# Attention and MLP on one core: q and k's maxima turned by VectorE and transfers from step 16 on, kv products of two units in one row

## The chip, the cores and the metric

The kernel runs on one core of a Trainium2 chip. The metric is device microseconds of that core, the median of three runs. A core has TensorE (PE in the profile; its weight loads are PEld), VectorE (DVE), ScalarE (ACT), GpSimd (POOL) and SyncE (SP), which issues most of the transfers here. Each engine runs its own instructions in order and waits on semaphores for the others.

## The reference

For each of 8 batches and 8 heads (sequence 576, head dimension 64) the reference takes a softmax of q along the head dimension and a softmax of k along the sequence, and multiplies twice; the heads side by side are the rows of an MLP with 512 inputs, 2048 inner units and a squared ReLU:

```python
q_s = softmax over d of q            # max, exp, sum along the 64 of a row
k_s = softmax over s of k            # max, exp, sum along the 576 rows
kv  = einsum('bhsd,bhse->bhde', k_s, v)
x   = einsum('bhsd,bhde->bhse', q_s, kv)        # then (B*S, H*D) = (4608, 512)
h = x @ w_in ; r = max(h, 0) ; out = (s * r * r + b) @ w_out
```

All of it is float32. Each float32 product of the MLP and of q with kv is made of three fp32r matmuls, of a high and a low part: high by high, high by low, low by high.

## The kernel before

The MLP runs in 9 blocks of 512 tokens (8 batches, and a ninth block of the 64 left-over rows of each batch), each block in 16 steps, one for each 128 inner units. `g1(t)` makes h of step t (12 matmuls of 128x512 into one PSUM buffer, L600), and from it r, gh and gl: ACT takes the ReLU (L620), DVE squares and scales (L621), ACT rounds the high part gh (L622), DVE subtracts the low part gl (L613). `g2(t)` adds step t's part to the block's four accumulators (12 matmuls of 128x512, L674); it stands one step behind `g1`, so that PE has the order h(t), acc(t-1), h(t+1), acc(t). There is one h buffer and one r buffer, and two of gh and gl.

The attention is done in units of two heads, a pair of units at a time. The first 16 steps, with the first four pairs, are ordered by hand and by a planner; the change leaves them as they are, but for two small tiles with two buffers in place of four. From step 16 on `pair(pr)` writes out one pair after the other, 12 pairs in all, two to each of six blocks; `advance` hands its stages in between the steps (`STAGES` of them to a pair, spread over the first 13 steps of a block), and a scheduler sets each engine's order from that. The x that a block's two pairs make is used a block later.

A pair of before goes through PE in seven visits: two transposes that turn k's maxima (L469, `k_turn`), two that spread them over the partitions (L476, `spread`), twenty small matmuls for kv (L301, `heads`), and for each of the two units five transposes of q (L546) and six matmuls of q with kv (L563). DVE, ACT and POOL do the maxima, the exponentials, the sums and the splits into high and low parts between them. `held()` lets a DVE operation stand no earlier than behind the last gl. The input tiles k, q and v of these pairs have one buffer each; `loads(pr + 1)` is written behind the pair and fills them as they come free.

Of the kernel before, what the change touches and what calls it, by code (L numbers as in the profile page):

```python
# [8 lines left out]
F32 = mybir.dt.float32  # L9
# [17 lines left out]
def attention_moe(ctx: ExitStack, tc: tile.TileContext, q, k, v, w_in, w_out, s, b, out):  # L27
# [54 lines left out]
    def by_head(t):  # L82
        return t[:, 0:KQ].rearrange("p (h n d) -> p h n d", h=4, d=D)
# [4 lines left out]
    def v_tile(t):  # L88
        return t.rearrange("p (h n e) -> p h n e", h=4, n=NT)
# [316 lines left out]
    def q_stream(u):  # L406
# [79 lines left out]
    def k_exp(kt):  # L486
        nc.scalar.activation(kt, kt, AF.Exp)  # L487
        nc.gpsimd.memset(kt[LEFT:P, :, NQ], 0.0)

    def pair(pr):  # L490
        us = (2 * pr, 2 * pr + 1)
        bb = us[0] // NP
        kt, qt, vt = tiles.pop(pr)
        kt, qt, vt = by_head(kt), by_head(qt), v_tile(vt)
        kts, qts = [[t[:, 2 * i:2 * i + 2] for i in range(2)] for t in (kt, qt)]

        def sm(n):
# [34 lines left out]
        yield  # L532
        def normalize(i):
            u, qe = us[i], qes[i]
            qs = small.tile([P, NT, 2], F32, name=f"qs_{u}", tag="qs")
            nc.vector.tensor_reduce(out=qs, in_=qe, axis=AX.X, op=ALU.add)  # L536
            nc.vector.tensor_scalar(qs, qs, 1e-9, None, op0=ALU.add)
            qr = small.tile([P, NT, 2], F32, name=f"qr_{u}", tag="qr")
            nc.vector.reciprocal(qr, qs)  # L539
            nc.gpsimd.tensor_tensor(out=qe, in0=qe, in1=bc(qr, [P, NT, 2, D]), op=ALU.mult)  # L540

        def transpose(i):
            u, qe = us[i], qes[i]
            qT = ps.tile([P, 1024], F32, name=f"qT_{u}", tag="big")
            for n in range(NT):
                nc.tensor.transpose(qT[:, n * P:(n + 1) * P], qe[:, n, :, :].rearrange("p h d -> p (h d)"), ident)  # L546
            qh = work.tile([P, S], F32R, name=f"qh_{u}", tag="qh")
            ql = work.tile([P, S], F32R, name=f"ql_{u}", tag="ql")
            split(qT[:, 0:S], qh, ql, nc.scalar.copy, nc.vector)
            terms = ((kvhl[:, 0, i], qh), (kvhl[:, 0, i], ql), (kvhl[:, 1, i], qh))  # L550
            return terms

        def product(i, terms):
            u = us[i]
            hp = u % NP

            HB = TB // 2
            xh, xl = x_tile(bb)
            xp = ps.tile([P, 2, 512], F32, name=f"xp_{u}", tag="big")
            halves = [xp[:, 0], xp[:, 1]]  # L560
            for a, (t, src) in enumerate(zip(halves, (slice(0, HB), slice(HB, S)))):
                for j, (lhs, rhs) in enumerate(terms):
                    nc.tensor.matmul(  # L563
                        t[:, 0:src.stop - src.start], lhs, rhs[:, src], start=(j == 0), stop=(j == len(terms) - 1)
                    )
                if a == 1:
                    keep_left(u, t[:, HB:HB + LEFT])
            hl = [t[:, hp, :].rearrange("p (a c) -> p a c", a=2) for t in (xh, xl)]
            split(xp[:, :, 0:HB], hl[0], hl[1], nc.scalar.copy, nc.vector)
# [269 lines left out]
```

## Time and profile before

| | |
|---|---|
| median of 3 runs | 901.12 us (900.09 to 901.48) |
| the profiled execution | 900.48 us, its span 898.7 us |
| PE busy | 876.0 us, 97% of the span, 4528 matmuls |
| DVE, ACT, POOL busy | 51%, 40%, 9% |
| TensorE clock granted | 0.997 of full speed |

The page gives busy time by engine, the span in 40 slices, the transfers, the chain of work that ended last, and the costliest groups of instructions with the idle time before them. The views read beside it are the windows (busy time by stretch), the chain in order of time, the timeline of a stretch, and the groups of one engine. A busy PE is modelled (matmuls overlap), so distances between starts say more than durations.

### The profile page before, as it was taken

Reading aid. Unit: us, or ns where it says so; the run is one execution under the profiler, and the core shown is the slowest. Engines: PE = TensorE matmul, PEld = TensorE weight load, DVE = VectorE, ACT = ScalarE, POOL = GpSimd, SP = SyncE. Lnnn points to the kernel's source line nnn. Section 1 sums busy time; section 2 is a strip of 40 time slices with the busy share of each in tenths; the row PEclk is TensorE's granted clock in tenths of the full one; section 3 lists DMA queues with packets and bytes.
Section 4 is the critical chain, followed back from the end, with each engine's and each line's share of the span. In section 5 each row is a group of like instructions: output and inputs, shape, how many; then the busy total and the mean of one; then the engine's idle time right before and its main releaser. Section 6 shows DMA issues by size and latency. Waiting matters only on the chain.

```text
span 898.7 us, 11364 instructions
## 1 busy us (share of the span) xinstructions
PE 876.0 (97%) x4528; PEld 721.8 (80%) x4528; DVE 459.5 (51%) x723; ACT 357.4 (40%) x564; POOL 83.6 (9%) x110
## 2 busy tenths in 40 slices
PE   4899999999999999999999999999999999999997
PEld 3577778888888888888888888888888888888886
DVE  6999975563364536353636345554545332223222
ACT  5999863342233333242334333333333322222222
POOL 1000001110020202020102002110202100000000
PEclk9999999999999999999999999999999999999999
DMA  9977211303130303030130213031300110001001
GB/s 241 305 258 240 72 39 50 80 5 81 47 80 4 80 19 109 5 80 3 48 79 18 69 47 80 4 80 47 83 4 1 50 47 1 1 1 47 1 1 47
DMA packets 82308, 57.35 MB, mean 64 GB/s; under 512 B 52944, under 2 KB 77520, under 8 KB 82128
## 3 DMA queue, kind: packets, MB, share of 16 engines
q1 hardware_dynamic: 80848, 55.52, 21.7%
q10 hardware_dynamic: 1408, 1.12, 0.4%
q8 instruction: 35, 0.57, 0.3%
q14 instruction: 17, 0.14, 0.1%
HBM read 46.14 MB, written 10.49 MB: 63 GB/s over the span
## 4 chain that ended last, share of the span: by engine, by line
PE 89%; DVE 4%; ACT 3%; DMA 2%; SPq 1%; issue 1%; ACTq 0%; DVEq 0%
PE h L600 41%; PE acc L674 41%; PE xp L563 2%; PE kv L301 2%; PE qT L546 1%; ACT low L202 1%; DMA raw<-in_q_dram 1%; DVE w L225 1%; ACT st L205 1%; DMA k<-in_k_dram 1%; PE xp L443 0%; DMA q<-in_q_dram 0%; ACT r L633 0%; DVE low L218 0%; DVE st L215 0%
## 5 line engine op out<-in xcount | busy, mean ns | idle before, releaser
L600 PE MATMUL h<-x,w 128*128 128x512 f32 x1728 | 428.9, 393 | 2.3 <-ACT r L633 1.6
L600 PEld LDWEIGHTS h<-x,w 128*128 128x128 f32 x1728 | 321.9, 188 | 70.5 <-ACT r L633 3.4
L674 PE MATMUL acc<-w,gh 128*128 128x512 f32 x1152 | 340.6, 392 | 0.0
L674 PEld LDWEIGHTS acc<-w,gh 128*128 128x128 f32 x1152 | 215.1, 188 | 44.3 <-ACT o L687 0.4
L621 DVE SCALAR_TENSOR_TENSOR r<-r,sb 128x512 f32<-128x512 f32 x128 | 102.0, 797 | 277.2 <-ACT r L620 277.1
L674 PE MATMUL acc<-w,gl 128*128 128x512 f32 x576 | 207.7, 392 | 0.5 <-DVE gl L643 0.5
L620 ACT ACTIVATE r<-h 128x512 f32<-128x512 f32 x128 | 76.5, 597 | 302.6 <-PE h L600 293.0
L613 DVE SCALAR_TENSOR_TENSOR gl<-r,sb,gh 128x512 fp32r<-128x512 f32 x132 | 102.6, 777 | 84.6 <-ACT gh L622 84.2
L622 ACT ACTIVATE gh<-r,sb 128x512 fp32r<-128x512 f32 x128 | 92.7, 724 | 94.3 <-DVE r L621 93.6
L674 PEld LDWEIGHTS acc<-w,gl 128*128 128x128 f32 x576 | 108.1, 188 | 23.7 <-DVE gl L643 1.4
L521 POOL TENSOR_TENSOR q<-q,qm 128x640 f32<-128x640 f32 x24 | 30.3, 1262 | 442.6 <-DVE qm L520 441.3
L540 POOL TENSOR_TENSOR qe<-qe,qr 128x640 f32<-128x640 f32 x24 | 30.6, 1275 | 49.2 <-DVE qr L539 45.0
L487 ACT ACTIVATE k<-k 128x640 f32<-128x640 f32 x28 | 20.4, 736 | 20.1 <-DVE k L480 20.1
L523 ACT ACTIVATE qe<-q 128x640 f32<-128x640 f32 x24 | 17.5, 731 | 21.9 <-POOL q L521 21.9
L536 DVE TENSOR_REDUCE qs<-qe 128x10 f32<-128x640 f32 x24 | 19.6, 817 | 12.7 <-ACT qe L523 12.7
L480 DVE TENSOR_TENSOR k<-k,mb 128x640 f32<-128x640 f32 x28 | 21.9, 816 | 7.3 <-PE mb L476 7.3
L102 DVE TENSOR_TENSOR x<-xp,x 128x512 fp32r<-128x512 f32 x24 | 16.6, 690 | 16.9 <-ACT x L101 16.9
L102 DVE TENSOR_TENSOR ql<-qT,qh 128x576 fp32r<-128x576 f32 x24 | 18.2, 757 | 11.6 <-ACT qh L101 11.6
L563 PE MATMUL xp<-qh,kvhl 128*128 128x256 f32 (+1 forms) x96 | 23.4, 297 | 0.0
L101 ACT CAST qh<-qT 128x576 fp32r<-128x576 f32 x24 | 15.4, 641 | 18.7 <-PE qT L546 18.7
L301 PEld LDWEIGHTS kv<-v,k 128*64 128x64 f32 x600 | 19.4, 141 | 4.2 <-issue 2.0
L301 PE MATMUL kv<-v,k 128*64 128x65 f32 (+1 forms) x600 | 21.4, 228 | 0.0
(101 smaller groups left out, 519.8 us busy)
## 6 DMA issues: line engine op xcount, KB each, us to landing
st<-in_moe_w_in_dram SPq DMA_DIRECT2D x16, 512.0 KB, 7.7
st<-in_moe_w_out_dram SPq DMA_DIRECT2D x16, 512.0 KB, 8.5
out_dram<-o SPq DMA_DIRECT2D x16, 512.0 KB, 2.7
q<-in_q_dram SPq DMA_DIRECT2D x14, 512.0 KB, 4.6
k<-in_k_dram SPq DMA_DIRECT2D x14, 512.0 KB, 5.0
v<-in_v_dram SPq DMA_DIRECT2D x56, 128.0 KB, 4.7
xleft<-xleft SPq DMA_DIRECT2D x16, 64.0 KB, 1.7
xleft_all<-xleft SPq DMA_DIRECT2D x1, 1024.0 KB, 4.7
```

Of the source, the lines that this page charges most:

```text
L102: return eng_l.tensor_tensor(out=l, in0=src, in1=h.bitcast(F32), op=ALU.subtract)
L301: nc.tensor.matmul(kv[h * D:(h + 1) * D, i], kt[:, i, h, n], vt[:, 2 * i + h, n], start=(n == 0), stop=(n == NT - 1))
L480: nc.vector.tensor_tensor(out=kt, in0=kt, in1=mb[:, i * P:(i + 1) * P].rearrange("p (h d) -> p h d", h=2).unsqueeze(2).to_broadcast([P, 2, ...
L521: nc.gpsimd.tensor_tensor(out=qt, in0=qt, in1=bc(qm, [P, 2, NT, D]), op=ALU.subtract)
L540: nc.gpsimd.tensor_tensor(out=qe, in0=qe, in1=bc(qr, [P, NT, 2, D]), op=ALU.mult)
L563: nc.tensor.matmul(t[:, 0:src.stop - src.start], lhs, rhs[:, src], start=(j == 0), stop=(j == len(terms) - 1))
L600: nc.tensor.matmul(hp_, w[:, j, c, :], x[:, c, :], start=(c == 0 and i == 0), stop=(c == NP - 1 and i == 2))
L613: gls.append(nc.vector.scalar_tensor_tensor(out=gl, in0=r, scalar=b_col, in1=gh.bitcast(F32), op0=ALU.add, op1=ALU.subtract))
L620: nc.scalar.activation(r, hp_, AF.Relu)
L621: nc.vector.scalar_tensor_tensor(out=r, in0=r, scalar=s_col, in1=r, op0=ALU.mult, op1=ALU.mult)
L622: nc.scalar.activation(gh, r, AF.Identity, bias=b_col)
L674: last = nc.tensor.matmul(a, g[:, js], w_, start=(f == 0 and i == 0), stop=(f == NFC - 1 and i == 2)).ins
```

## The change

Five things change in a pair from step 16 on.

- k's maxima: DVE turns the maxima over a partition's rows in blocks of 32x32 (`k_out`), reduces them, and SP writes 4 KB to DRAM and reads it back, spread over all 128 partitions as a tile of 128x1024 (`k_in`, 512 KB). DVE joins the four parts (`k_join`) and subtracts (`k_under`). The four transposes on PE are gone.
- q: the exponentials are written in another order, so that DVE turns q in blocks of 32x32 (`turn`), SP writes the turned tile to DRAM (320 KB) and reads it back in two transfers of 64 partitions each (`fetch_q`). The ten transposes on PE are gone.
- The split of q into high and low parts (`parts`) reads SBUF in place of PSUM, 128x640 in place of 128x576, and the low part overwrites the tile.
- The products of kv and q (`products`) of both units are written in one row, behind both splits, into one pair of PSUM banks and the small buffer; the q side is read in runs of 32 elements.
- The stages stand in another order (k's maxima out, q's work, k's subtraction, kv, products), and there are 11 in place of 13.

The core of the diff:

```diff
+    maxima = {}
+    def k_max_0(pr, kt):
+        m2, m1, _ = k_tiles(pr)
+        k_max_2(kt, m2)
+        m2s, ks = [t.rearrange("p h n (r t) -> p h n t r", t=2) for t in (m2, kt)]
+        m1 = m1.rearrange("p h (t r) -> p h t r", t=2)
+        nc.vector.tensor_tensor(out=m1, in0=m2s[:, :, 0], in1=m2s[:, :, 1], op=ALU.max)
+        nc.vector.tensor_tensor(out=m1[0:LEFT], in0=m1[0:LEFT], in1=ks[0:LEFT, :, NQ], op=ALU.max)
+        return m2, m1
+    def k_out(pr, m2, m1):
+        m = m2.rearrange("p h n d -> p (h n d)")[:, 0:4 * D]
+        nc.vector.transpose(out=m, in_=m1.rearrange("p h t r -> p (h t r)"))
+        top = small.tile([P, 4, 2], F32, name=f"top_{pr}", tag="top", bufs=1)
+        nc.vector.tensor_reduce(out=top, in_=m.rearrange("p (h t c) -> p h t c", h=4, t=2), axis=AX.X, op=ALU.max)
+        maxima[pr] = dram.tile([4, P, 2], F32, name=f"maxima_{pr}", tag="maxima", bufs=2)
+        nc.sync.dma_start(maxima[pr].rearrange("h p t -> p h t"), top)
+    def k_in(pr):
+        mb = work.tile([P, 4, 4, D], F32, name=f"mb_{pr}", tag="tmp", bufs=NTMP)
+        src = maxima.pop(pr).rearrange("h p t -> (h p t)").partition_broadcast(P)
+        nc.sync.dma_start(mb.rearrange("p h a d -> p (h a d)"), src)
+        return mb
+    def k_join(mb):
+        mb = mb.rearrange("p h a d -> p h (a d)")
+        for n in (2 * D, D):
+            nc.vector.tensor_tensor(out=mb[:, :, 0:n], in0=mb[:, :, 0:n], in1=mb[:, :, n:2 * n], op=ALU.max)
+        return mb[:, :, 0:D]
+    def k_under(kt, mb):
+        nc.vector.tensor_tensor(out=kt, in0=kt, in1=mb.unsqueeze(2).to_broadcast([P, 2, NT, D]), op=ALU.subtract)
+    SQ = 32
+    turned = {}
     def pair(pr):
         us = (2 * pr, 2 * pr + 1)
         bb = us[0] // NP
-        kt, qt, vt = tiles.pop(pr)
-        kt, qt, vt = by_head(kt), by_head(qt), v_tile(vt)
+        kt, qraw, vt = tiles.pop(pr)
+        kt, qt, vt = by_head(kt), by_head(qraw), v_tile(vt)
         kts, qts = [[t[:, 2 * i:2 * i + 2] for i in range(2)] for t in (kt, qt)]
+        qes = []
         def sm(n):
             return ps.tile([P, 512], F32, name=f"{n}_{pr}", tag="sm", bufs=1)
-        m2, m1, km = k_tiles(pr)
-        with held():
-            k_max_2(kt, m2)
-        k_max_1(kt, m2, m1)
-        yield
-        kT = sm("kT")
-        k_turn(m1, kT)
-        k_top(kT, km)
-        yield
-        mb = spread(km, sm("mb"))
-        for i in range(2):
-            k_less(kts[i], mb, i)
-            k_exp(kts[i])
-            yield
-
-        qes = []
-        for i in range(2):
+        def q_exp(i):
             u, qt = us[i], qts[i]
             qm = small.tile([P, 2, NT], F32, name=f"qm_{u}", tag="qm")
             with held():
                 nc.vector.tensor_reduce(out=qm, in_=qt, axis=AX.X, op=ALU.max)
             nc.gpsimd.tensor_tensor(out=qt, in0=qt, in1=bc(qm, [P, 2, NT, D]), op=ALU.subtract)
-            qe = work.tile([P, NT, 2, D], F32, name=f"qe_{u}", tag="qe", bufs=2)
-            nc.scalar.activation(qe.rearrange("p n h d -> p h n d"), qt, AF.Exp)
+            qe = work.tile([P, 2, 2, NT, SQ], F32, name=f"qe_{u}", tag="qe", bufs=2)
+            nc.scalar.activation(qe, qt.rearrange("p h n (r t) -> p h t n r", t=2), AF.Exp)
             qes.append(qe)
+        def normalize(i):
+            u, qe = us[i], qes[i]
+            qs = small.tile([P, 2, 2, NT], F32, name=f"qs_{u}", tag="qs", bufs=2)
+            nc.vector.tensor_reduce(out=qs, in_=qe, axis=AX.X, op=ALU.add)
+            nc.vector.scalar_tensor_tensor(
+                out=qs[:, :, 0], in0=qs[:, :, 0], scalar=1e-9, in1=qs[:, :, 1], op0=ALU.add, op1=ALU.add
+            )
+            qr = small.tile([P, 2, 2, NT], F32, name=f"qr_{u}", tag="qr", bufs=2)
+            nc.vector.reciprocal(qr, qs[:, :, 0].unsqueeze(2).to_broadcast([P, 2, 2, NT]))
+            qe = qe.rearrange("p h t n r -> p (h t n) r")
+            qr = qr.rearrange("p h t n -> p (h t n)").unsqueeze(2).to_broadcast([P, 4 * NT, SQ])
+            nc.gpsimd.tensor_tensor(out=qe, in0=qe, in1=qr, op=ALU.mult)
+        def turn(i):
+            u, qe = us[i], qes[i]
+            tb = qraw[:, i * NT * P:(i + 1) * NT * P]
+            nc.vector.transpose(out=tb, in_=qe.rearrange("p h t n r -> p (h t n r)"))
+            turned[u] = dram.tile([2, P, 2 * NT * SQ], F32, name=f"turned_{u}", tag="turned", bufs=2)
+            nc.sync.dma_start(turned[u].rearrange("h p e -> p h e"), tb.rearrange("p (h e) -> p h e", h=2))
+        def fetch_q(i):
+            u = us[i]
+            qT = work.tile([P, NT * P], F32, name=f"qT_{u}", tag="qe", bufs=2)
+            src = turned.pop(u).rearrange("h (a r) (t e) -> h (r t) a e", r=SQ, t=2)
+            for h in range(2):
+                nc.sync.dma_start(qT[h * D:(h + 1) * D].rearrange("p (a e) -> p a e", e=NT * SQ), src[h])
+            qes[i] = qT
+        def parts(i):
+            u, qT = us[i], qes[i]
+            qh = work.tile([P, NT * P], F32R, name=f"qh_{u}", tag=("qh", "ql")[i])
+            ql = qT.bitcast(F32R)
+            split(qT, qh, ql, nc.scalar.copy, nc.vector)
+            qh, ql = [t.rearrange("p (s a n c) -> p s n a c", s=2, a=2, c=SQ) for t in (qh, ql)]
+            return ((kvhl[:, 0, i], qh), (kvhl[:, 0, i], ql), (kvhl[:, 1, i], qh))
+        def products(terms):
+            xh, xl = x_tile(bb)
+            xp, xq = ps.tile([P, 2, 512], F32, name=f"xp_{pr}", tag="big"), sm("xq")
+            halves = [(xp[:, 0], xp[:, 1, 0:TB // 2]), (xq, xp[:, 1, TB // 2:TB])]
+            for i in range(2):
+                for a, (t, n) in enumerate(zip(halves[i], (NT, NQ))):
+                    for j, (lhs, rhs) in enumerate(terms[i]):
+                        nc.tensor.matmul(
+                            t[:, 0:n * D], lhs, rhs[:, a, 0:n], start=(j == 0), stop=(j == len(terms[i]) - 1)
+                        )
...
+        with held():
+            m2, m1 = k_max_0(pr, kt)
+        k_out(pr, m2, m1)
+        yield
+        mb = k_in(pr)
+        for i in range(2):
+            q_exp(i)
+            yield
+        normalize(0)
+        turn(0)
+        yield
+        normalize(1)
+        turn(1)
+        fetch_q(0)
+        yield
+        mb = k_join(mb)
+        for i in range(2):
+            k_under(kts[i], mb[:, 2 * i:2 * i + 2])
+            k_exp(kts[i])
+            if i:
+                fetch_q(1)
             yield
...
-        def normalize(i):
-            u, qe = us[i], qes[i]
...
-        def transpose(i):
-            u, qe = us[i], qes[i]
-            qT = ps.tile([P, 1024], F32, name=f"qT_{u}", tag="big")
-            for n in range(NT):
-                nc.tensor.transpose(qT[:, n * P:(n + 1) * P], qe[:, n, :, :].rearrange("p h d -> p (h d)"), ident)
...
-        def product(i, terms):
...
+        terms = []
         for i in range(2):
-            normalize(i)
+            terms.append(parts(i))
             yield
-            t = transpose(i)
-            yield
-            product(i, t)
-            yield
+        products(terms)
+        yield
     G = {}
@@ -699,7 +770,7 @@
     NU = B * NP
     NBLK = B + 1
     NSTEP = NBLK * NFC
-    STAGES = 13
+    STAGES = 11
     tiles = {}
     def transfers():
```

What the scheduler made of it is seen at three places. All are in the second pair of the block whose accumulators end in 3686 before and in 3705 now.

PE, around that pair's kv. Before (mb spreads k's maxima, qT turns q, kv is the small product, h and acc are the MLP):

```order
L476 MATMUL mb_4009<-ident,km_3969 128x128 x2
L600 MATMUL h_4122<-x_3090,w_876 128x512 x12
L674 MATMUL acc_0_3686<-w_864,gh_4069 128x512 x2
L674 MATMUL acc_2_3693<-w_864,gh_4069 128x512 x2
L546 MATMUL qT_4160<-ident,qe_4053 128x128 x5
L301 MATMUL kv_4092<-v_93,k_91 64x65 x20
L674 MATMUL acc_0_3686<-w_864,gl_4070 128x512
```

Now, the same stretch:

```order
L671 MATMUL h_4089<-x_3146,w_864 128x512 x12
L301 MATMUL kv_4164<-v_93,k_91 64x65 x10
L745 MATMUL acc_0_3705<-w_796,gh_4050 128x512 x2
L745 MATMUL acc_2_3712<-w_796,gh_4050 128x512 x2
L301 MATMUL kv_4164<-v_93,k_91 64x65
L745 MATMUL acc_0_3705<-w_796,gl_4051 128x512
L745 MATMUL acc_0_3705<-w_796,gh_4050 128x512 x2
L745 MATMUL acc_0_3705<-w_796,gl_4051 128x512
L745 MATMUL acc_2_3712<-w_796,gl_4051 128x512
L745 MATMUL acc_2_3712<-w_796,gh_4050 128x512 x2
L745 MATMUL acc_2_3712<-w_796,gl_4051 128x512
L301 MATMUL kv_4164<-v_93,k_91 64x65 x3
```

The transposes mb and qT are gone, and kv is spread over three visits (a fourth follows) between the MLP's matmuls.

DVE, from the step before k's subtraction to the gl behind it. Before (km is the reduction of the turned maxima in PSUM, mb the spread maxima, qs and qr q's sums and their reciprocals):

```order
L621 SCALAR_TENSOR_TENSOR r_4028<-r_4028,sb 128x512 [waits Activation_49]
L613 SCALAR_TENSOR_TENSOR gl_4030<-r_4028,sb,gh_4029 128x512 [waits PE_49,Activation_49]
L520 TENSOR_REDUCE qm_4050<-q_92 128x10 [waits DMAHW2_49,DMAHW1_49]
L472 TENSOR_REDUCE km_3969<-kT_3993 128x2 [waits PE_49]
L536 TENSOR_REDUCE qs_4142<-qe_4053 128x10 [waits Activation_49]
L621 SCALAR_TENSOR_TENSOR r_4068<-r_4068,sb 128x512 [waits Activation_49]
L537 TENSOR_SCALAR qs_4142<-qs_4142 128x10 [waits DVE_49]
L539 RECIPROCAL qr_4145<-qs_4142 128x10 [waits DVE_49]
L480 TENSOR_TENSOR k_91<-k_91,mb_4009 128x640 [waits PE_49]
L480 TENSOR_TENSOR k_91<-k_91,mb_4009 128x640
L613 SCALAR_TENSOR_TENSOR gl_4070<-r_4068,sb,gh_4069 128x512 [waits Activation_49]
```

Now (mb is the tile that a transfer brings; top, the reduction whose transfer precedes it, stands just ahead of r and gl of the step before these rows):

```order
L546 TENSOR_REDUCE qm_4014<-q_92 128x10 [waits DMAHW2_49,DMAHW1_49]
L546 TENSOR_REDUCE qm_4031<-q_92 128x10
L520 TENSOR_TENSOR mb_4012<-mb_4012 128x4x128 [waits DMAHW4_49]
L520 TENSOR_TENSOR mb_4012<-mb_4012 128x4x64 [waits DVE_49]
L524 TENSOR_TENSOR k_91<-k_91,mb_4012 128x640 [waits DVE_49]
L524 TENSOR_TENSOR k_91<-k_91,mb_4012 128x640
L556 TENSOR_REDUCE qs_4056<-qe_4017 128x20 [waits Activation_49]
L692 SCALAR_TENSOR_TENSOR r_4049<-r_4049,sb 128x512 [waits Activation_49]
L556 TENSOR_REDUCE qs_4077<-qe_4034 128x20 [waits Activation_49]
L557 SCALAR_TENSOR_TENSOR qs_4056<-qs_4056 128x2x5 [waits DVE_49]
L557 SCALAR_TENSOR_TENSOR qs_4077<-qs_4077 128x2x5 [waits DVE_49]
L684 SCALAR_TENSOR_TENSOR gl_4051<-r_4049,sb,gh_4050 128x512 [waits PE_49,Activation_49]
```

The wait of the subtraction has moved from PE to a transfer's semaphore (DMAHW), two joins stand ahead of it, and behind it in the queue stand q's sums, r and gl of the MLP's step.

SP, from that pair's first transfer on. Before (xleft is a store, the rest are loads of the next pair):

```order
L244 DMA xleft<-xleft_3863 128x2x64 [waits DMAHW2_49,Activation_49]
L284 DMA v_93<-in_v_dram 128x4x64 [waits DMAHW3_49,PE_49]
L284 DMA v_93<-in_v_dram 128x4x64 [waits DMAHW6_49,DMAHW4_49,PE_49]
L274 DMA k_91<-in_k_dram 128x4x256 [waits DMAHW5_49,PE_49,Activation_49]
L275 DMA k_91<-in_k_dram 64x4x64 [waits DVE_49,PE_49]
L274 DMA q_92<-in_q_dram 128x4x256 [waits DMAHW7_49,Activation_49]
L275 DMA q_92<-in_q_dram 64x4x64 [waits DMAHW0_49]
```

Now (maxima and turned are DRAM tiles, mb and qT what is read back from them):

```order
L509 DMA maxima_3990<-top_3988 128x4x2 [waits DMAHW3_49,DVE_49]
L514 DMA mb_4012<-maxima_3990 128x1024 [waits DMAHW4_49,DMAHW3_49]
L284 DMA v_93<-in_v_dram 128x4x64 [waits DMAHW5_49,PE_49]
L284 DMA v_93<-in_v_dram 128x4x64 [waits DMAHW6_49,PE_49]
L572 DMA turned_4063<-q_92 128x2x320 [waits DMAHW7_49,DVE_49]
L572 DMA turned_4084<-q_92 128x2x320 [waits DMAHW0_49,DVE_49]
L579 DMA qT_4086<-turned_4063 64x4x160 [waits DMAHW1_49,DMAHW7_49,Activation_49,Pool_49]
L579 DMA qT_4086<-turned_4063 64x4x160 [waits DMAHW2_49]
L579 DMA qT_4149<-turned_4084 64x4x160 [waits DMAHW0_49,Activation_49,Pool_49]
L579 DMA qT_4149<-turned_4084 64x4x160 [waits DMAHW4_49]
L274 DMA q_92<-in_q_dram 128x4x256 [waits DMAHW5_49]
L275 DMA q_92<-in_q_dram 64x4x64 [waits DMAHW6_49]
```

Eight transfers are new, the loads of k and q of the next pair stand behind them, and two loads of v, which wait for PE's kv, stand ahead of the turned q.

## Rows read from the trace of the kernel before

**Rows 1.** The page: busy time (us, share, instructions), and PE and its clock in slices

```profile
PE 876.0 (97%) x4528; PEld 721.8 (80%) x4528; DVE 459.5 (51%) x723; ACT 357.4 (40%) x564; POOL 83.6 (9%) x110
...
PE   4899999999999999999999999999999999999997
...
PEclk9999999999999999999999999999999999999999
```

**Rows 2.** Windows: busy us of each engine, PEclk, DMA share and GB/s of a stretch

```profile
300.00:400.00 100.00, 100.00 (x532) 83.12 (x531) 47.60 (x80) 34.19 (x57) 14.24 (x16) 1.00 0.21 57
```

**Rows 3.** The chain in order of time: start us, us, what

```profile
353.05 2.93 PE h L600 x12
...
449.79 2.93 PE h L600 x12
...
727.30 2.72 PE h L600 x12
...
814.34 2.72 PE h L600 x12
```

**Rows 4.** Timeline of PE around a pair: start us, us, line, operation

```profile
337.47 0.62 PE L674 MATMUL acc<-w,gh 128*128 128x512 f32 x2
...
340.20 0.38 PE L469 MATMUL kT<-ident,m 128*128 128x128 f32 x2
...
343.18 1.07 PE L674 MATMUL acc<-w,gh 128*128 128x512 f32 x4
344.09 0.39 PE L674 MATMUL acc<-w,gl 128*128 128x512 f32 x1
...
345.45 0.38 PE L476 MATMUL mb<-ident,km 128*128 128x128 f32 x2
...
346.13 2.89 PE L600 MATMUL h<-x,w 128*128 128x512 f32 x12
...
355.82 1.08 PE L674 MATMUL acc<-w,gh 128*128 128x512 f32 x4
356.74 0.71 PE L546 MATMUL qT<-ident,qe 128*128 128x128 f32 x5
...
359.13 2.89 PE L600 MATMUL h<-x,w 128*128 128x512 f32 x12
```

**Rows 5.** Timeline of one step: from h's end to gl, all engines

```profile
439.92 1.07 PE L674 MATMUL acc<-w,gh 128*128 128x512 f32 x4
...
440.12 0.60 ACT L620 ACTIVATE r<-h 128x512 f32<-128x512 f32 x1 [3.56 <-PE h L600]
...
442.30 0.75 DVE L613 SCALAR_TENSOR_TENSOR gl<-r,sb,gh 128x512 fp32r<-128x512 f32 x1 [0.79 <-ACT gh L622]
```

**Rows 6.** Groups of DVE, by shape: count, busy us, mean ns, idle before

```profile
L621 DVE SCALAR_TENSOR_TENSOR r<-r,sb 128x512 f32<-128x512 f32 x128 | 102.0, 797 | 277.2 <-ACT r L620 277.1
L480 DVE TENSOR_TENSOR k<-k,mb 128x640 f32<-128x640 f32 x28 | 21.9, 816 | 7.3 <-PE mb L476 7.3
...
L520 DVE TENSOR_REDUCE qm<-q 128x10 f32<-128x640 f32 x24 | 19.4, 812 | 0.0
...
L461 DVE TENSOR_TENSOR m<-k 128x512 f32<-128x512 f32 x14 | 9.6, 689 | 2.8 <-PE xp L563 2.8
...
L464 DVE TENSOR_TENSOR m<-m 128x256 f32<-128x256 f32 x14 | 5.9, 418 | 0.0
```

**Rows 7.** The page: transfers issued, KB each, median us from issue to landing

```profile
out_dram<-o SPq DMA_DIRECT2D x16, 512.0 KB, 2.7
q<-in_q_dram SPq DMA_DIRECT2D x14, 512.0 KB, 4.6
k<-in_k_dram SPq DMA_DIRECT2D x14, 512.0 KB, 5.0
...
xleft<-xleft SPq DMA_DIRECT2D x16, 64.0 KB, 1.7
xleft_all<-xleft SPq DMA_DIRECT2D x1, 1024.0 KB, 4.7
```

More of the change, by code (lines that the diff above doesn't have):

```diff
@@ L421, in q_stream @@
         yield Op("DVE", 0.73, due)
-        qs = small.tile([P, NT, 2], F32, name=f"qs_{u}", tag="qs")
+        qs = small.tile([P, NT, 2], F32, name=f"qs_{u}", tag="qs", bufs=2)
         nc.vector.tensor_reduce(out=qs, in_=qe, axis=AX.X, op=ALU.add)
@@ L425, in q_stream @@
         nc.vector.tensor_scalar(qs, qs, 1e-9, None, op0=ALU.add)
-        qr = small.tile([P, NT, 2], F32, name=f"qr_{u}", tag="qr")
+        qr = small.tile([P, NT, 2], F32, name=f"qr_{u}", tag="qr", bufs=2)
         nc.vector.reciprocal(qr, qs)
@@ new lines, in parts @@
+        def parts(i):
[15 more added lines that the diff above has]
+                        )
+            for i, u in enumerate(us):
+                keep_left(u, halves[i][0][:, NQ * D:NT * D])
+                hl = [t[:, u % NP].rearrange("p (n s c) -> p s n c", n=NQ, s=2) for t in (xh, xl)]
+                if i == 0:
+                    x = xp[:, :, 0:NQ * D].rearrange("p s (n c) -> p s n c", n=NQ)
+                    split(x, *hl, nc.scalar.copy, nc.vector)
+                else:
+                    for a in range(2):
+                        x = halves[i][a][:, 0:NQ * D].rearrange("p (n c) -> p n c", n=NQ)
+                        split(x, *[t[:, a] for t in hl], nc.scalar.copy, nc.vector)
@@ L532, in pair @@
         yield
-        def normalize(i):
-            u, qe = us[i], qes[i]
[L535 to L540, printed above, removed]
-        def transpose(i):
-            u, qe = us[i], qes[i]
-            qT = ps.tile([P, 1024], F32, name=f"qT_{u}", tag="big")
-            for n in range(NT):
-                nc.tensor.transpose(qT[:, n * P:(n + 1) * P], qe[:, n, :, :].rearrange("p h d -> p (h d)"), ident)
[L547 to L551, printed above, removed]
-        def product(i, terms):
[L554 to L569, printed above, removed]
+        terms = []
         for i in range(2):
-            normalize(i)
+            terms.append(parts(i))
             yield
-            t = transpose(i)
-            yield
-            product(i, t)
-            yield
+        products(terms)
+        yield
     G = {}
```

## Prediction

> **What bounds the kernel now.** I read the page's busy times first. PE is busy for 97% of the span, no other engine for more than 51%, and the clock granted is full in every slice [rows 1]. A busy PE is modelled, so the second view was the windows: from 300 to 400 us, between the start-up and the tail, PE has no idle time at all, while DVE works 48 us, ACT 34 and POOL 14 of the hundred, and the 16 DMA engines are used for 21% [rows 2]. The third was the chain of waits in order of time, for its distances. The step that holds a pair's kv starts at 353.05 and, one block later, at 449.79: 96.74 us for a block of 16 steps with two pairs. Where no attention is left, 16 steps from 727.30 to 814.34 take 87.04 us, 5.44 a step, 2.72 for each dozen matmuls of 512 columns [rows 3]. So two pairs cost a block 9.70 us, 4.85 each, and all of it is PE's own work: what goes from PE goes from the time, as long as nothing else makes PE wait.
>
> **What the change removes.** Only PE's transposes count. The timeline gives their price as the stretch of the MLP around them grows [rows 4]. From acc at 337.47 to the next acc at 343.18 are 5.71 us in place of 5.44: kT costs 0.27. From there to h at 346.13 are 2.95 in place of 2.72: mb costs 0.23. From acc at 355.82 to h at 359.13 are 3.31 in place of 2.72: five qT cost 0.59. A pair has kT and mb once and qT twice: 0.27 + 0.23 + 2 x 0.59 = 1.68 us. The other 3.17 of the 4.85 are kv and the products, which keep their 20 and 12 matmuls of the same columns. Twelve pairs save 12 x 1.68 = 20.2 us; a block would take 87.04 + 2 x 3.17 = 93.4.
>
> The Trainium skill (VectorE: DVE Perf Modes, sections The three transpose paths and Rules for kernel authors) speaks against the change: it tells one to transpose 128x128 on TensorE if PSUM will do, since VectorE turns 32x32 blocks only, and it prices TensorE's transpose at 390 ns and VectorE's at 311 for bf16. By its price 168 transposes would be worth 65 us, an estimate from that page; in this trace five cost 0.59, and the measurement decides. Its advice weighs an operation by itself, and here PE is full and DVE half empty.
>
> **What it adds, and what hides it.** DVE gets, in a pair, two transposes of 128x640 and one of 128x256, which no row shows; I take the nearest rows of the same shape, 0.81 and 0.42 [rows 6], and as ends nothing and double that. With two joins (0.69 and 0.42) this is 3.2 us a pair, 38 in all, beside a DVE that idles half the time. ACT's and POOL's passes stay, ACT's splits 640 columns wide in place of 576. SP gets eight transfers a pair, about 1.8 MB. The start-up keeps its order; two buffers in place of four for small sums that one engine writes and reads in order cost nothing. None of this is on PE, but DVE, ACT and SP take things in order, so a late transfer holds back the MLP's r, gh and gl behind it. That is the risk, and it needs a timetable.
>
> The slack of a step: ReLU starts 0.20 after the end of h (439.92, where the next matmul starts), and gl ends 2.93 later, at 443.05, so 3.13 after h [rows 5]. PE wants gh 5.44 after h, and gl four matmuls later, 0.91 [rows 4].
>
> The second pair of a block is the tight one. Its zero is the start of h in the step whose gl stands ahead of the maxima; PE then does h, acc, h, acc, h to 13.60, acc, and h to 19.04, ten of kv (half of the some 1.5 us), and wants gh of the third h from 19.8 and its gl from 20.8.
> - The first gl ends at 2.72 + 3.13 = 5.85. Three maxima, the transpose and the reduction (0.69 and four of 0.42) end at 8.2. Now D: the maxima's 4 KB out to DRAM, 512 KB back.
> - D is unknown from both sides. The write moves less than xleft's 64 KB (1.7 us), but in pieces of 8 bytes; stores of 512 KB take 2.7 [rows 7]. I take 2.0. The read is 512 KB in rows of 4 KB with SP's traffic thin: xleft_all, alone, takes 4.7 for twice as much, loads of 512 KB in a crowd 4.6 and 5.0, stores 2.7. I take 3.0, nearest the lone ones. With 0.2 for the hand-overs D is 5.2, from 1.7 + 2.7 = 4.4 to 2.7 + 5.0 + 0.2 = 7.9.
> - At 8.2 + 5.2 = 13.4 the joins start; DVE would have come to them at about 12.9 (gl of the second h, two maxima of q). Joins 1.1, two subtractions 1.6, one sum of q 0.8: at 16.9 r of the third h (0.8), the second sum of q and small ones (1.2), gl (0.8): done at 19.7, that is 14.5 + D. PE wants it at 20.8. So PE waits from D = 6.3 on.
>
> The first pair of a block has the same chain with the subtraction one step earlier in relation to its kv: maxima done at about 10.8 from the end of the block's first h, then joins, subtractions, one transpose (3.6), r (0.8), gh (0.7), 15.9 + D against 23.3, where PE comes from kv: from D = 7.4 on.
>
> The turned q goes out and back in 5.3 as I take it (store of 320 KB 2.2; two reads of 160 KB, issued 0.5 apart, 2.6), at most 2.7 + 0.6 + 5.0 = 8.3. ACT's split (qh) waits for it ahead of a gh: in the second pair DVE's transpose ends at about 22, q is back at 27.3, gh done at 28.8 against acc's start at 31.4; in the first pair the margins are 2.3 to 2.6. PE waits from 7.6 on. A transpose at double price eats 0.4 of the margin of D, and 0.8 of that of q.
>
> The moving side of the products is read in runs of 32 elements where all rows of before read whole ones. I take no cost; if it halved the rate, a pair would lose its 1.6 us of products once more.
>
> So at the values taken PE never waits, and the profiled execution falls from 900.48 to 880.3. It lies 0.64 under the median of before, 901.12; the median forecast is 901.12 - 20.2 = 880.9.
>
> **The rivals.** (a) The transfers come late within the bounds: at D = 7.9 the second pair's PE waits 1.6 and the first's 0.5, six blocks lose 12.6; with q's trip at 8.3 another 0.7 in each of twelve pairs, 8. The time lies between 883 and 901, at the middle about 889. For it speak the 4.6 and 5.0 of the loads [rows 7], against it that those go out three to a row, as the order shows, and this read goes alone.
>
> (b) Slower than before: 128 partitions read the same 4 KB. No row here shows a wide read of one small place. If it is served slowly, DVE stands at the join, and r, gh and gl of the MLP stand behind it. A block loses (D - 6.3) + (D - 7.4); it has saved 3.36. From D = 8.5, a read of 6.3 us, the change loses. At a read of 8 us (66 GB/s) D is 10.2, a block loses 6.7, and the time is 880.9 + 40 = 921. Against it speaks that nothing in the trace is served that slowly.
>
> The Trainium skill (DMA: Bandwidth & Descriptors, section Latency and other measured facts) has rows at a pitch of several MiB drop from over 200 to 103 GB/s, and supposes that streams meet in one HBM channel. At 103 the read would move its data in 5.1 us, an estimate from that page, which is about (b)'s point of decision; no run here shows it.
>
> (c) The runs of 32 slow the products: 12 x 1.64 = 19.7 back, 900.6, no change. Nothing in the profile speaks for it but that the form is new.
>
> (d) The transposes leave PE, but the scheduler's order makes PE wait elsewhere, so that the change doesn't give what it removes. The order shows kv and the products in more pieces between the MLP's matmuls; at 0.1 for a break this is 2 to 4 us: 883 to 885. It is counted with (a).
>
> **How the numbers follow.** No wait: 0.62, 879 to 882.5 (the sum, with 1.5 for what prices read from single stretches may miss). (a) and (d): 0.20. (b): 0.14, of which 0.02 ends within 0.2% of before. (c): 0.04, mostly the same. A measurement of this kernel tells about 0.2%, 1.8 us, from no change. Faster: 0.62 + 0.19 = 0.81; the same: 0.01 + 0.02 + 0.03 = 0.06; slower 0.13. The range takes the first case and three quarters of (a): 878.5 to 895. The likeliest case's own is 879 to 882.5.
>
> **What would show it.** Right: 4360 matmuls; from one block's kv to the next 93.4 us in place of 96.7; no wait of PE for gh, gl, or k in these blocks; DVE's first join of a pair waiting on its transfer for under 1 us; maxima landing in about 2 and mb in about 3. Wrong: PE idle ahead of acc, released by gh or gl, once or twice a block, with the join's idle time on DVE several us long (a or b), or ACT's qh late and gh behind it (a, by q); products of over 1.64 a pair with no wait (c).

## The result and the profile after

The changed kernel takes 903.60 us (median of 20 runs, 901.69 to 908.38) where the kernel before takes 900.65 beside it (20 runs). The ratio is 1.0035, 95% interval [1.0026, 1.0044]: slower by a third of a per cent, and no run of after is as fast as the slowest of before (901.59). Forecast were 880.9 and a range of 878.5 to 895. The profiled execution of after took 905.46, a little above the median.

The page of after, and below it the answer on transfers for 130 to 730 us (issues, KB each, median us to landing):

```profile
PE 868.5 (96%) x4360; PEld 704.1 (78%) x4360; DVE 495.3 (55%) x795; ACT 360.2 (40%) x576; POOL 86.2 (10%) x110
...
PEclk9999999999999999999999999999999999999999
```

```profile
turned<-q SPq DMA_DIRECT2D x24, 320.0 KB, 2.3
qT<-turned SPq DMA_DIRECT2D x48, 160.0 KB, 3.1
...
mb<-maxima SPq DMA_DIRECT2D x12, 512.0 KB, 4.1
...
maxima<-top SPq DMA_DIRECT2D x12, 4.0 KB, 3.1
```

The 168 matmuls are gone (4528 in [rows 1]), yet PE's busy time fell by 7.5 us only and the span rose. The maxima's write takes 3.1 and the read 4.1, where 2.0 and 3.0 had been taken.

PEclk is 9 in every slice, but a slice is 22.6 us long and a 9 stands for 90% or more. Finer windows (columns as in the windows below) and PE's timeline show that TensorE's clock fell once in the first pair of a block:

```profile
357.00:359.50 2.50, 0.86 (x5) 0.41 (x4) 1.49 (x2) 1.43 (x3) 0.00 (x0) 1.00 0.33 117
359.75:363.00 3.25, 3.25 (x9) 2.52 (x8) 1.15 (x4) 0.50 (x2) 0.00 (x0) 0.50 0.90 248
```

```profile
358.49 0.74 PE L745 MATMUL acc<-w,gh 128*128 128x512 f32 x2 [1.48 <-ACT gh L693]
...
359.80 1.05 PE L745 MATMUL acc<-w,gh 128*128 128x512 f32 x2
```

PE had waited 1.48 us for gh. The clock granted is then 0.50 for some 3.4 us, the lower of its two levels (1.2 in place of 2.4 GHz), and two matmuls of acc take 1.05 where they take 0.62 in [rows 4]. That costs about 1.7 us, an estimate: half of 3.4. Of the 20 runs the ten with a mean granted clock of 0.999 or more take 901.7 to 904.1, the other ten 902.8 to 908.4. So the clock explains part of the spread, and the change is slower at the full clock too.

The windows, one block from the h of one first pair's kv step to the next (us, then busy us of PE, PEld, DVE, ACT, POOL, the clock, DMA share, GB/s):

```profile
451.79:548.20 96.41, 95.11 (x490) 77.68 (x488) 52.95 (x89) 33.90 (x57) 12.73 (x14) 1.00 0.32 88
```

Before, the block took 96.74 [rows 3]; here 96.41, with 1.3 us in which PE is idle; before there was none [rows 2]. The mean of the six blocks of after, by the same distances (the last over its 16 steps), is 97.5; forecast were 93.4. So 3.3 us are saved in a block and 4.1 come back. The waits name who is late (us in total, times, longest):

```profile
PE acc L745 <- ACT gh L693: 9.6, 13, 1.5
...
PE acc L745 <- DVE gl L684: 1.0, 6, 0.2
...
DVE mb L520 <- DMA mb<-maxima: 33.7, 12, 3.8
...
ACT qh L101 <- DMA qT<-turned: 42.4, 21, 4.0
```

The timeline of a second pair of a block shows the first of two places (start us, us, engine, line, operation, idle time before; kv's twenty matmuls have two records each):

```profile
475.32 0.37 SPq L509 DMA_DIRECT2D maxima<-top  x1
...
477.48 0.75 DVE L684 SCALAR_TENSOR_TENSOR gl<-r,sb,gh 128x512 fp32r<-128x512 f32 x1 [0.79 <-ACT gh L693]
...
478.35 0.33 SPq L514 DMA_DIRECT2D mb<-maxima  x1
...
482.52 1.15 DVE L520 TENSOR_TENSOR mb<-mb 128x512 f32<-128x512 f32 x2 [2.83 <-DMA mb<-maxima]
...
485.92 0.74 DVE L692 SCALAR_TENSOR_TENSOR r<-r,sb 128x512 f32<-128x512 f32 x1
486.07 0.81 PE L301 MATMUL kv<-v,k 128*64 128x65 f32 x20
486.69 0.72 ACT L693 ACTIVATE gh<-r,sb 128x512 fp32r<-128x512 f32 x1 [0.65 <-DVE r L692]
...
487.46 1.19 PE L745 MATMUL acc<-w,gh 128*128 128x512 f32 x4 [0.58 <-ACT gh L693]
488.58 0.33 PE L301 MATMUL kv<-v,k 128*64 128x65 f32 x2
...
490.88 0.45 PE L301 MATMUL kv<-v,k 128*64 128x65 f32 x6
```

From the write's issue to the join are 7.2 us (7.0 to 8.5 in the twelve pairs). DVE stands 2.83 at the join, with r of the MLP behind it; so gh comes late, and PE is idle for 0.58 although half of kv has been put in front. In a first pair the trip of the maxima is 7.6 long, and the second place shows behind it:

```profile
442.98 0.38 SPq L509 DMA_DIRECT2D maxima<-top  x1
446.00 0.33 SPq L514 DMA_DIRECT2D mb<-maxima  x1
447.16 0.37 SPq L572 DMA_DIRECT2D turned<-q  x1
...
450.53 1.15 DVE L520 TENSOR_TENSOR mb<-mb 128x512 f32<-128x512 f32 x2 [2.50 <-DMA mb<-maxima]
451.45 1.25 SPq L579 DMA_DIRECT2D qT<-turned  x2
...
455.13 0.73 ACT L101 CAST qh<-qT 128x640 fp32r<-128x640 f32 x1 [1.08 <-DMA qT<-turned]
455.77 0.72 ACT L693 ACTIVATE gh<-r,sb 128x512 fp32r<-128x512 f32 x1
456.54 0.73 PE L745 MATMUL acc<-w,gh 128*128 128x512 f32 x2 [0.55 <-ACT gh L693]
```

The read of mb and the store of the turned q run beside each other; the store takes 4.3 (to the issue at 451.45) where the median is 2.3. So q is back 8.0 after its first issue, ACT stands at qh, gh stands behind it, and PE waits.

### The profile page after: what moved, and what is told of

It is laid out like the page before. It is cut to its first block, busy times and chain, and to the rows that moved or that the text cites. A ratio compares the mean times of both kernels' runs of the same rounds, so it can differ in the third digit from the quotient of the medians.

```text
span 903.7 us, 11413 instructions
## 1 busy us (share of the span) xinstructions
PE 868.5 (96%) x4360; PEld 704.1 (78%) x4360; DVE 495.3 (55%) x795; ACT 360.2 (40%) x576; POOL 86.2 (10%) x110
## 4 chain that ended last, share of the span: by engine, by line
PE 63%; DVE 15%; DMA 14%; ACT 3%; issue 3%; SPq 2%; ACTq 0%; DVEq 0%
PE acc L745 30%; PE h L671 29%; DMA mb<-maxima 4%; DMA maxima<-top 3%; DMA turned<-q 2%; DMA qT<-turned 2%; PE xp L600 2%; DVE r L692 2%; DVE k L524 1%; DVE w L225 1%; DVE gl L684 1%; DVE qs L556 1%; ACT gh L693 1%; DVE mb L520 1%; DMA v<-in_v_dram 1%
## 5 line engine op out<-in xcount | busy, mean ns | idle before, releaser
L745 PE MATMUL acc<-w,gh 128*128 128x512 f32 x1152 | 344.2, 394 | 9.6 <-ACT gh L693 9.6
L745 PE MATMUL acc<-w,gl 128*128 128x512 f32 x576 | 211.3, 394 | 1.9 <-DVE gl L684 1.0
L684 DVE SCALAR_TENSOR_TENSOR gl<-r,sb,gh 128x512 fp32r<-128x512 f32 x132 | 99.7, 756 | 65.1 <-ACT gh L693 64.9
L102 DVE TENSOR_TENSOR qT<-qT,qh 128x640 fp32r<-128x640 f32 x24 | 19.8, 825 | 39.9 <-ACT qh L101 39.9
L101 ACT CAST qh<-qT 128x640 fp32r<-128x640 f32 x24 | 17.5, 728 | 42.6 <-DMA qT<-turned 42.4
L520 DVE TENSOR_TENSOR mb<-mb 128x512 f32<-128x512 f32 (+1 forms) x24 | 13.3, 556 | 34.1 <-DMA mb<-maxima 33.7
L301 PE MATMUL kv<-v,k 128*64 128x65 f32 (+1 forms) x600 | 25.5, 226 | 0.2 <-ACT k L487 0.2
L102 POOL TENSOR_TENSOR kvhl<-kvf,kvhl 128x256 fp32r<-128x256 f32 x12 | 8.9, 741 | 120.6 <-ACT kvhl L101 55.3
L570 DVE STREAM_TRANSPOSE q<-qe 128x640 f32<-128x640 f32 x24 | 20.0, 832 | 0.4 <-POOL qe L564 0.4
```

The source lines that it names most:

```text
L102: return eng_l.tensor_tensor(out=l, in0=src, in1=h.bitcast(F32), op=ALU.subtract)
L301: nc.tensor.matmul(kv[h * D:(h + 1) * D, i], kt[:, i, h, n], vt[:, 2 * i + h, n], start=(n == 0), stop=(n == NT - 1))
L520: nc.vector.tensor_tensor(out=mb[:, :, 0:n], in0=mb[:, :, 0:n], in1=mb[:, :, n:2 * n], op=ALU.max)
L684: gls.append(nc.vector.scalar_tensor_tensor(out=gl, in0=r, scalar=b_col, in1=gh.bitcast(F32), op0=ALU.add, op1=ALU.subtract))
L745: last = nc.tensor.matmul(a, g[:, js], w_, start=(f == 0 and i == 0), stop=(f == NFC - 1 and i == 2)).ins
```

## The experiments

Three theories: **T1**, the maxima's trip is late; **T2**, q's trip is late by itself; **T3**, kv in four visits costs PE time by itself. **R**, the rival to all: the loss is spread, by 22 MB more of transfers (against it speaks that a step without attention takes 5.44 us in after, as before). Times are medians; ratios are to before, in runs on the same chip. Before takes 899.8 to 900.7 on these chips, so a difference of under 1 us from after's 903.6 says nothing.

### Later join

```diff
-        mb = k_join(mb)
+        with held():
+            mb = k_join(mb)
```

> The changed kernel with one edit: VectorE comes to the join of the maxima of the second pair of a block only behind the MLP's next gl, as the other held operations do; the order of the first pair stays, and nothing is left out. The changed kernel takes 97.5 us a block where 93.4 were forecast. T1 (the maxima's trip, 7.2 us in place of 5.2, makes VectorE stand at the second pair's join with r and gl of the MLP behind it; there PE loses 0.6 to 1 us, and the product of k and v is broken into four visits because of it, which costs about 1 us more): both go, 2.0 to 2.3 us a block, six blocks: 903.6 falls to 890 to 892, and the first pair's wait for gh (about 1.5 us a block) stays. T2 (the turned q comes late, ScalarE's split stands ahead of gh): under 3 us. R (the rival: the loss is spread, since more than 20 MB more of transfers slow everything): no change, 902 to 904.

892.76, ratio 0.9908 [0.9895, 0.9921], 0.8 above T1's range. T1 holds in the main; R falls, and T2 as the only cause. In the second pair kv comes in two visits, and no wait for gh is left there. The first pair's stays; the waits:

```profile
PE acc L746 <- ACT gh L694: 5.3, 7, 1.5
```

### Later splits of q

```diff
-    gls = []
+    gls, ghs = [], []
...
-            split(qT, qh, ql, nc.scalar.copy, nc.vector)
+            with held(), tc.issue_after(ghs[-1].ins):
+                split(qT, qh, ql, nc.scalar.copy, nc.vector)
...
-        nc.scalar.activation(gh, r, AF.Identity, bias=b_col)
+        ghs.append(nc.scalar.activation(gh, r, AF.Identity, bias=b_col))
```

> The changed kernel with one edit: ScalarE's and VectorE's splits of the turned q (qh, ql) come behind the next gh and gl of the MLP in place of ahead of them; nothing is left out. T2 (in the first pair of a block q's trip of about 8 us keeps ScalarE at qh, and gh of the MLP stands behind it; PE loses 1 to 1.5 us there): the first pair's kv step goes from 8.4 to about 7 us, six blocks: 903.6 falls to 895 to 898. T1 (the maxima's trip alone): no more than 2 us less. R (spread loss by the transfers): no change, 902 to 904.

894.87, ratio 0.9941 [0.9929, 0.9953], as T2 said but for 0.1 us: the first pair's kv step takes 7.4 in place of 8.6 in the mean, while the second pair's stays above 8. That ACT's place behind the transfer costs PE time is shown; whether q's trip is late by itself is not.

### Both

The two edits together.

> The changed kernel with both edits: the second pair's join behind the next gl, and the splits of the turned q behind the next gh and gl; nothing is left out. T1 and T2 together say that no wait is left to PE: a block is 93.4 to 94.0 us and the time 881 to 885, what was forecast for the change itself, so faster than before (900.7) by 2%. If waits move on to the next thing that is late (kv itself behind a late join, products behind late splits) it lies between 885 and 895. R (spread loss by the transfers, matmuls slower beside them): 900 or more.

885.16, ratio 0.9835 [0.9822, 0.9847], at the upper end of what T1 and T2 said together. Four of six blocks take 93.9 us, and PE waits for gh twice, 1.0 in all.

### kv in a row

```diff
-    gls = []
+    gls, pes = [], []
...
-        heads(kv, kt.rearrange("p (u h) n d -> p u h n d", u=2), vt)
+        with tc.issue_after(pes[-1]):
+            heads(kv, kt.rearrange("p (u h) n d -> p u h n d", u=2), vt)
...
                     ).ins
+                pes.append(last)
```

> The changed kernel with one edit: kv of every pair stands in one row behind an acc of the MLP, so that the second pair's twenty matmuls are one visit in place of four; the transfers and the joins stay where they are. T3 (four visits cost about 1 us more than one, by themselves): the second pair's steps lose 1 us, 903.6 falls to about 898. T1 (visits are only PE's filling of the time in which it would wait for gh): the 0.95 us of the visits turns into a longer wait of acc for gh, 0.6 becomes 1.4 us in the second pair, and the time stays within 2 us of 903.6.

906.01, ratio 1.0057 [1.0038, 1.0076]: no gain, 2.4 above after. The wait of acc for gh grew from 9.6 to 15.1:

```profile
PE acc L746 <- ACT gh L694: 15.1, 12, 2.6
```

As long as gh is late, a visit of kv is work that stands in PE's wait; T3 alone is wrong. The 0.4 us by which the time leaves T1's "no change" are the clock's, as far as can be told: in the profiled execution (908.46) it is 0.50 in three stretches of some 3 us, each behind a wait for gh of 1.7 to 2.6, and the one of six runs with a mean of 0.999 took 901.23, just under the fastest of after.

### k's part alone, q's part alone

k's part in the kernel before (`k_out` and `k_in` are those of the change), and its removal from the changed kernel; the first maxima and the subtraction go with them (`k_max_0`, `k_under`):

```diff
...
-        k_max_1(kt, m2, m1)
+        k_out(pr, m2, m1)
         yield
-        kT = sm("kT")
-        k_turn(m1, kT)
-        k_top(kT, km)
+        mb = k_in(pr)
         yield
-        mb = spread(km, sm("mb"))
+        mb = k_join(mb)
...
-            k_less(kts[i], mb, i)
+            k_under(kts[i], mb[:, 2 * i:2 * i + 2])
```

```diff
...
-        k_out(pr, m2, m1)
+        k_max_1(kt, m2, m1)
         yield
-        mb = k_in(pr)
+        kT = sm("kT")
+        k_turn(m1, kT)
+        k_top(kT, km)
...
-        mb = k_join(mb)
+        mb = spread(km, sm("mb"))
...
-            k_under(kts[i], mb[:, 2 * i:2 * i + 2])
+            k_less(kts[i], mb, i)
```

> The kernel before with one part of the change: k's maxima go through VectorE's transpose, DRAM and back; q is transposed on TensorE as before; nothing is left out. It saves PE kT and mb, 0.50 us a pair, 6 us in all: 894.7 if nothing waits. T1 (the trip takes 7.2 us): VectorE has here only an r and a gl between its reduction and the join, so it stands at every join with the next gl behind it, 4 to 5 us long, more than a step's slack: PE loses 1 to 2.5 us in each of twelve pairs, 12 to 30 us, and the time is 905 to 925, slower than before. R (the trip hides, only q's part costs): 894 to 897.

> The changed kernel with k's maxima on TensorE as before (kT, mb) and the turned q, the products in a row and the shorter stages kept; nothing is left out. It saves PE the five qT of each unit, 1.18 us a pair, 14.2 in all: 886.5 if nothing waits. T2 (q's trip of about 8 us keeps ScalarE's split ahead of gh in the first pair of a block, 1.5 us a block): 893 to 897. T1 alone, with no loss by q: 886 to 889.

k's part alone: 914.43, ratio 1.0163 [1.0149, 1.0177], as T1 said. DVE waits at every join, and what it holds back here is gl, k's subtraction and through them q's work:

```profile
451.74 1.15 DVE L519 TENSOR_TENSOR mb<-mb 128x512 f32<-128x512 f32 x2 [3.25 <-DMA mb<-maxima]
452.81 0.74 DVE L646 SCALAR_TENSOR_TENSOR gl<-r,sb,gh 128x512 fp32r<-128x512 f32 x1
...
461.44 0.76 PE L579 MATMUL qT<-ident,qe 128*128 128x128 f32 x5 [1.67 <-POOL qe L573]
```

q's part alone: 892.80, ratio 0.9917 [0.9904, 0.9931]. The time is just under T2's range, but not for T2's reason: its waits have no row of PE for gh in the attention's blocks, although ACT stands 59.1 us at qh. A block takes 95.3 to 95.5 in four of six; 1.0 of what it has over 93.4 is kT and mb, and most of the rest is kv in three visits. So q's trip is hidden when the maxima's trip is not beside it: the first trip in a block's first pair takes 6.0 to 7.2 here, 7.5 to 8.3 in after, and T2 is a consequence of T1.

### Wider pieces

The maxima lie in DRAM by partition: 128 rows of 32 bytes in place of 512 pieces of 8. The join's second maximum puts them in order; `k_join` is rewritten for that and not shown.

```diff
-        maxima[pr] = dram.tile([4, P, 2], F32, name=f"maxima_{pr}", tag="maxima", bufs=2)
-        nc.sync.dma_start(maxima[pr].rearrange("h p t -> p h t"), top)
+        maxima[pr] = dram.tile([P, 4, 2], F32, name=f"maxima_{pr}", tag="maxima", bufs=2)
+        nc.sync.dma_start(maxima[pr], top)
...
-        src = maxima.pop(pr).rearrange("h p t -> (h p t)").partition_broadcast(P)
+        src = maxima.pop(pr).rearrange("p h t -> (p h t)").partition_broadcast(P)
...
```

> The changed kernel with one edit: the 4 KB of maxima lie in DRAM by partition, so they are written as 128 rows of 32 bytes in place of 512 pieces of 8 (the read back is the same 4 KB for each partition, the join sorts them); nothing is left out. W1 (the write's 3.1 us is the price of its small pieces): it lands in 2.0 or less, the trip is about 6.1, below the 6.3 from which the second pair's PE waits; 903.6 falls to 895 to 899. W2 (the price is a fixed time of any write, whatever its pieces): 2.8 to 3.1, and the time stays within 2 us of 903.6.

890.22, ratio 0.9887 [0.9873, 0.9900]: 13.4 under after, more than W1 said; W2 falls. Eleven of the twelve writes land in 1.4 to 1.5 us; the first takes 3.1, and makes the longest wait of DVE below. Why is open. The transfers, and what DVE still waits for:

```profile
mb<-maxima SPq DMA_DIRECT2D x12, 512.0 KB, 3.6
...
maxima<-top SPq DMA_DIRECT2D x12, 4.0 KB, 1.4
```

```profile
DVE mb L520 <- DMA mb<-maxima: 5.1, 7, 1.2
```

The same second pair as above, with the engines' order unchanged:

```profile
464.11 0.34 SPq L509 DMA_DIRECT2D maxima<-top  x1
...
465.64 0.33 SPq L514 DMA_DIRECT2D mb<-maxima  x1
...
469.30 1.55 DVE L520 TENSOR_TENSOR mb<-mb 128x512 f32<-128x512 f32 x1 [0.83 <-DMA mb<-maxima]
...
474.33 0.73 ACT L696 ACTIVATE gh<-r,sb 128x512 fp32r<-128x512 f32 x1 [0.65 <-DVE r L695]
474.86 0.80 PE L301 MATMUL kv<-v,k 128*64 128x65 f32 x20
...
475.59 1.21 PE L748 MATMUL acc<-w,gh 128*128 128x512 f32 x4
476.73 0.33 PE L301 MATMUL kv<-v,k 128*64 128x65 f32 x2
...
479.03 0.45 PE L301 MATMUL kv<-v,k 128*64 128x65 f32 x6
```

From write to join are 5.2 us, gh starts ahead of kv, and acc follows without idle time. The first pair's kv step takes 6.99 in five of six blocks; the forecast's prices give 5.44 + 3.17 - 1.64 = 6.97. With the read done earlier, the store of the turned q behind it takes 2.3 in four of the six, where it took 3.8 to 4.4 in after.

### Both and wider pieces

The three edits together.

> The version with the later join and the later splits (885.2 us), and the maxima written as rows of 32 bytes; nothing is left out. In that version PE waits for gh only twice, 0.4 to 0.6 us, and the first pair's step of kv takes 1 us more in two of six blocks. W1 (the write becomes 1 us shorter): these go, 883 to 884.5. W2 (fixed time): 885 as it is.

882.63, ratio 0.9808 [0.9794, 0.9821], just under W1's range: the best here, better than both kernels. Every block takes 93.85, and PE is never idle in it:

```profile
438.44:532.29 93.85, 93.85 (x489) 77.72 (x488) 53.84 (x89) 33.38 (x57) 12.55 (x14) 1.00 0.32 90
```

### Wider pieces, kv in a row

The edit of the kv row, on the two versions with wider pieces.

> The changed kernel with maxima written as rows of 32 bytes (890.2 us, no wait of PE for gh left) and, besides, the product of k and v of every pair in one row; nothing is left out. In that version the second pair's four steps around kv take 26.2 us, 1.3 more than the first pair's 24.9, and their twenty instructions come in four visits. T3 (each visit between the MLP's matmuls has a price, some 0.3 to 0.4 us): with the visits gone and no wait to take their place, the second pair comes to 25.0 us, and the time falls by 6 x 1.2 = 7 to 883. T1 (visits only fill time in which PE would wait): it waits again, and the time stays within 2 us of 890.

> The version with the later join, the later splits and rows of 32 bytes (882.6 us), and the product of k and v behind an acc of the MLP; nothing is left out. The second pair's twenty come still in two visits of ten, one at either side of that pair's next weights, where one row is not to be had. T3 by visits: no visit goes, so no change, 881.5 to 883.5.

The first: 887.38, ratio 0.9856 [0.9840, 0.9873], 2.8 under the version with wider pieces alone, between what T3 and T1 said. The four steps from the second pair's kv on fall from 26.2 to 25.5 in the two quietest blocks, with a wait of 0.18 for gh left in them; in others acc waits for gh and the products for kv's split (1.5 and 1.4 us in all). The second: 883.07, ratio 0.9811 [0.9796, 0.9825], the same as without the edit, since the visits are the same.

## Why the prediction was wrong

**What held.** PE was the bound, and what goes from PE goes from the time as long as nothing makes it wait: where no wait is left, a block takes 93.85 against 93.4 forecast, and the time is 882.6 against 880.9. So the price of the removed transposes, 1.68 us a pair, stands; the rival (c) fell, since a first pair's products take 7.07 - 5.44 = 1.63 us as before. DVE's transpose of 128x640 takes 0.83 where 0.81 was taken. The bounds too from which PE waits, D = 6.3 and 7.4, served: at some 5 nearly nothing waits, at 7.0 to 8.5 it does (in the second pair for gh, where the timetable has gl come last). The rival (b) is not what happened: the same 4 KB are served to 128 partitions at up to 393 GB/s (below).

**The step that failed** is the value of D in the timetable of the second pair: "I take 2.0" for the write and "I take 3.0" for the read, D = 5.2. Measured were 3.1 and 4.1 in the median, and 7.0 to 8.5 for D. The write lies outside its own bounds, 1.7 to 2.7, because they came from stores in long rows; that this one goes "in pieces of 8 bytes" was written down, and given no price. The run with pieces of 32 bytes shows the price, 1.7 us; without it D is 4.7 to 5.3 in eleven of twelve pairs, and the second pair's wait is gone, with every engine's order unchanged. Of the 22.7 us between 903.6 and 880.9, this alone is 13.4. Whether the size of the pieces or their number (512 against 128) has the price, no run tells.

**What hung on it.** The formula behind the timetable gives 1.1 and 0.4 a block in the mean of the twelve D, 8.8 us in all. It takes each trip by itself. In the trace the late read ran into the store of the turned q and made its trip 8.0, above the 7.6 from which ACT's split holds back gh. The first pair lost 1.6 us a block there, the largest loss; 1.2 of it goes when ACT's order is changed, and all of it, in five of six blocks, when the read comes earlier. That trip was taken too low as well: 5.3 in the prediction, 6.0 to 7.1 in sixteen of the eighteen cases without the maxima's read beside it.

**The second term mis-sized** is (d): 0.1 us for a break of kv. Where nothing waits, the four steps from a pair's kv on take 26.2 us with four visits and 25.0 with one (a second and a first pair, wider pieces), 25.3 with two (both and wider pieces); the windows have the columns of those above, and PE is busy throughout:

```profile
472.05:498.27 26.22, 26.22 (x150) 20.91 (x149) 15.93 (x28) 10.50 (x19) 4.08 (x5) 1.00 0.44 121
441.65:466.61 24.96, 24.96 (x150) 20.80 (x149) 13.64 (x25) 9.76 (x18) 1.14 (x3) 1.00 0.42 107
```

```profile
474.32:499.65 25.33, 25.33 (x149) 20.88 (x148) 12.66 (x22) 9.67 (x18) 1.14 (x3) 1.00 0.43 113
```

So a break costs some 0.4, and 1.3 us a block in after, 7.6 in six, where (d) said 2 to 4; some 0.2 of the 1.3 are the products' own pieces. The 7.6 us from 890.2 to 882.6 are mostly this (6 x 0.9 = 5.4). A break is a cost only when PE has no wait to fill with it. The Trainium skill (TensorEngine Tiling (Array Packing), section Key Properties) says that a change of the tiling mode drains TensorE; kv runs as `128*64` and the MLP as `128*128` in the rows above, so each visit has two such changes. The trace agrees in sign, but no run here changes the mode alone.

**The clock** had no term: the prediction read it as full from slices in which a 9 stands for 90% or more. One fall in the six blocks of the profiled execution costs 0.3 us a block, and it came behind a wait that the prediction didn't have.

**By shares**, in the mean block of the profiled execution: 93.4 forecast, 1.3 for visits, 1.6 in the first pair's kv step (0.3 of it the clock), 0.8 in the second pair's, 0.4 at the products, 97.5. The records show 1.9 of the last three as idle time of PE. With wider pieces a block takes 94.7 to 95.2, so the last three hang mostly on the trip of the maxima.

The chance given to slower was 0.13, nearly all of it by a slow read. The case that came was (a) grown by its collision with q, and it was given no way beyond 901.

## What to carry to other kernels

A round trip through DRAM on the path of an engine that runs in order is priced piece by piece: look at how many pieces the write has, and of how many bytes, before its total, and at what else the queues carry when it lands. Give the wait room in the consumer's order (the join behind the next gl) before judging the edit: 18 of the 23 us came back by order alone, 13 by layout alone. Read the granted clock in a narrow window behind each long wait, not in the page's slices. And where removing work leaves other work in more pieces, the pieces belong in the sum.

## What the runs showed of the hardware

The transfers of a second pair, in slices of 0.25 us (busy tenths, GB/s); after, from 474 us on:

```profile
DMA  0020000007200000000000993279995200000000
GB/s 0 0 66 0 0 0 0 0 0 13 3 0 0 0 0 0 0 0 0 0 0 0 115 115 33 115 311 377 393 328 213 98 0 0 0 0 0 0 0 0
DMA packets 673, 0.54 MB, mean 54 GB/s; under 512 B 544, under 2 KB 544, under 8 KB 672
```

With wider pieces, from 464 us on:

```profile
DMA  0001100000749989441000000000000000000000
GB/s 0 0 0 6 10 0 0 0 0 0 131 82 360 442 311 410 131 148 66 16 0 0 0 0 0 0 0 0 0 0 0 0 0 0 0 0 0 0 0 0
DMA packets 288, 0.53 MB, mean 53 GB/s; under 512 B 160, under 2 KB 160, under 8 KB 288
```

In after, the write's bytes have moved by 476.75, but the read that waits for it is issued at 478.35, 1.6 us later. With pieces of 32 bytes the bytes have moved by 465.25 and the read goes out at 465.64, 0.4 later. The time of small pieces lies mostly behind the movement, not in it. The Trainium skill (DMA: Bandwidth & Descriptors, section Anatomy of one DMA — SWDGE (gpsimd) path) puts most of a transfer's fixed 2 us into the receipt of the last write. Here 1.6 of 3.0 us lie behind the movement with pieces of 8 bytes and 0.4 of 1.5 with 32, so the trace agrees for the first alone. Its fit of 2.0 us plus bytes at 436 GB/s is for transfers that GpSimd issues; SP issues these. It would give 2.0 for either layout of these 4 KB, and 5.2 for the trip, an estimate from that page, where 3.1 and 1.4, 7.2 and 5.2 were measured.

The read moves its 512 KB in ten slices, some 2.5 us, at up to 393 GB/s; the rest of its 4.1 lies ahead of the first byte and behind the last. It fell to 3.6 with the other layout although it moves the same bytes from the same 4 KB; why is left open.
